# One load of keys in six pieces: 2,688 columns as one load, the last 1,408 as 112 rows and four loads of 4 rows

## The chip, the cores and the metric

The kernel runs on one core of a Trainium2 chip. The metric is the device time of one execution in microseconds (us). Three runs of the kernel before gave 237.23, 237.36 and 237.38 us, a median of 237.36 us. The profile shows one further execution of the same program.

## The reference

One decoding step of a transformer block for two sequences (B = 2, one token each, width 512), in 32-bit floats:

```python
mod = (silu(c) @ w_mod)                      # six vectors of 512 a sequence: sa, ca, ga, sb, cb, gb
h = layernorm(x) * (1 + ca) + sa
q = h @ wq                                   # 32 heads of 128
k, v = k_cache[:, :, -4096:, :], v_cache[:, :, -4096:, :]   # 8 key/value heads, each used by 4 heads
o = softmax(q k^T / sqrt(128)) v
x = x + ga * (o @ wo)
h = layernorm(x) * (1 + cb) + sb
x = x + gb * (silu(h @ w1) @ w2)             # hidden width 1792
```

Only the last 4,096 positions of the caches count. For each of the 8 key/value heads `h` and each of the two sequences `b` that is one block of keys and one of values, of 4,096 x 128 floats, 2 MB each: 32 blocks, 64 MB. The weights are `w_mod` (6 MB), `wq` and `wo` (8 MB each), `w1` and `w2` (3.5 MB each).

## The kernel before

Every large input comes through one pool of eight tiles of 128 x 4,096 floats (`ring`, line 55), and every load is issued by SyncE, in the order of the program: `w_mod` in four loads, `wq` in four, then keys and values head by head, `wo` in four, a load of 4 KB (`x_sp`), `w1` in three and `w2` in five, the last of them 512 columns (256 KB). A block of keys or values is one load of 128 rows of 16 KB (lines 77 to 89): 32 consecutive positions lie in one partition.

The function `fetch(h)` issues the loads of one step: the keys of head `h` for both sequences, and then the values of head `h - 1` for both. The first lines of the loop (447 to 451) call it one step ahead. So the loads around the change are `k2_0, k2_1, v1_0, v1_1, k3_0, k3_1, v2_0, v2_1, k4_0, k4_1, v3_0, v3_1`, where `k3_1` is the keys of head 3 of sequence 1.

SyncE issues a load when two things hold: the tile of the ring is free again (its last reader has run), and the semaphore that the load will count up has been reached by the load that used it before. There are eight such semaphores for loads, given out in turn, so a load waits for the completion of the load eight places ahead of it. SyncE is one queue: what stands behind a waiting load waits too.

A load of 128 rows is spread over the core's 16 DMA engines, eight rows each. Each engine works through its rows in the order of the issues and writes one completion for each load; the load has landed when all 16 completions are there.

For each head VectorE turns the keys (`keys`, line 333: a `k` tile in four parts of 1,024 columns, and `keys(h, b, n4)` reads the columns from 1,024 `n4` on), TensorE forms the scores (line 349), VectorE and ScalarE form maximum and exponentials, and TensorE multiplies the turned probabilities with the values (`weighted`, line 416). TensorE and VectorE each keep the order of the program there. Behind the heads follow the output projection with `wo`, the second norm, `w1`, `w2`, and the store of the result.

Of the kernel before, what the change touches and what calls it, by code (L numbers as in the profile page):

```python
# [13 lines left out]
P = 128  # L14
# [9 lines left out]
def adaln_block(  # L24
# [21 lines left out]
    nc = tc.nc  # L46
    SK = k_cache.shape[2]
    W = min(4096, max(256, SK // 4))
# [20 lines left out]
    def stream(name):  # L69
        return ring.tile([P, 4096], F32, tag="st", name=name)  # L70
# [5 lines left out]

    def load_k(b, h):
        t = stream(f"k{h}_{b}")
        nc.sync.dma_start(
            t, k_cache[b, h, SK - W :, :].rearrange("(p n) d -> p (n d)", p=P)  # L80
        )
        return t

    def load_v(b, h):
# [239 lines left out]
    def fetch(h):  # L324

        if h < HKV:
            for b in range(B):
                kt[h, b] = load_k(b, h)
        if h > 0:
            for b in range(B):  # L330
                vt[h - 1, b] = load_v(b, h - 1)
# [352 lines left out]
```

## Time and profile before

| what | value |
|---|---|
| median of three runs | 237.36 us |
| the profiled execution's own time | 236.89 us |
| its span, first to last instruction | 235.0 us |
| bytes read from HBM | 97.53 MB, 415 GB/s over the span |
| TensorE / VectorE / ScalarE busy | 62% / 49% / 11% |
| mean granted TensorE clock | 0.87 |

The page of the profile cuts the span into 40 slices of 5.9 us and gives for each the busy share of the engines, of the 16 DMA engines and the rate in GB/s. The chain of work that ended last goes back from the last instruction to what released it. Times in the views are microseconds from the start of the span. A load's row in the queue's view stands at its issue; it lands some 30 us later.

### The profile page before, as it was taken

What the parts mean: (1) busy time and instruction counts of PE and PEld (TensorE: products, weight loads), DVE (VectorE), ACT (ScalarE), POOL (GpSimd) and SP (SyncE); (2) the same over time, 40 slices, a digit from 0 to 9 for tenths busy, and PEclk for the clock granted to TensorE, in tenths of its full rate; (3) what the DMA queues carried; (4) which work ended last, traced back from release to release, by engine and by line L of the source; (5) the groups of instructions that cost most, each with busy time, mean ns of one, the idle gap of its engine ahead of it and who ended that gap; (6) DMA issues with size and microseconds to landing.
All of it is one profiled execution on the core that took longest, in us unless ns stands there. A gap on an engine that the chain in (4) does not pass through costs nothing.

```text
span 235.0 us, 2644 instructions
## 1 busy us (share of the span) xinstructions
PE 146.5 (62%) x1094; PEld 45.9 (20%) x1094; DVE 114.6 (49%) x176; ACT 25.4 (11%) x56; POOL 10.3 (4%) x30
## 2 busy tenths in 40 slices
PE   0086546367187577667549519626743967788993
PEld 0032101101011121121112102111211222335332
DVE  0634000793694792693892792595298050002130
ACT  2200000100300200200200200200020021003210
POOL 8600000100000000000000000000000000000000
PEclk9999975759869997999976967965985799999999
DMA  6999999999999999999999999999999999999991
GB/s 253 426 438 427 427 438 427 424 439 427 429 441 424 427 438 427 429 438 424 429 435 429 427 432 432 432 429 432 428 429 429 429 432 429 432 426 422 421 412 56
DMA packets 7603, 97.69 MB, mean 416 GB/s; under 512 B 920, under 2 KB 936, under 8 KB 1576
## 3 DMA queue, kind: packets, MB, share of 16 engines
q1 hardware_dynamic: 7592, 97.54, 97.5%
q8 instruction: 8, 0.13, 0.2%
q14 instruction: 3, 0.02, 0.0%
HBM read 97.53 MB, written 0.00 MB: 415 GB/s over the span
## 4 chain that ended last, share of the span: by engine, by line
DMA 64%; DVE 22%; PE 10%; ACT 2%; issue 1%; SPq 1%; DVEq 0%
DVE kT L337 16%; DMA wo<-in_A_wo_dram 14%; DMA k<-in_A_k_cache_dram 14%; DMA v<-in_A_v_cache_dram 13%; DMA wq<-in_A_wq_dram 13%; DMA w<-in_B_w_dram 7%; PE s L349 5%; DMA wm<-in_w_mod_dram 3%; DVE zp L395 2%; PE o L423 2%; PE q L285 1%; DVE xp L393 1%; ACT pr L381 1%; DVE mx L359 1%; ACT L381 1%
## 5 line engine op out<-in xcount | busy, mean ns | idle before, releaser
L337 DVE STREAM_TRANSPOSE kT<-k 128x1024 f32<-128x1024 f32 x64 | 73.7, 1210 | 1.6 <-DMA k<-in_A_k_cache_dram 1.6
L349 PE MATMUL s<-kT,qbd 128*32 128x512 f32 x256 | 44.5, 670 | 11.2 <-DVE kT L337 11.1
L423 PE MATMUL o<-v,ptb 128*32 128x512 f32 x256 | 38.5, 730 | 19.8 <-DMA v<-in_A_v_cache_dram 19.3
L359 DVE TENSOR_REDUCE mx<-s 128x1 f32<-128x512 f32 x8 | 5.5, 691 | 40.1 <-PE s L349 40.1
L349 PEld LDWEIGHTS s<-kT,qbd 128*32 128x32 f32 x256 | 11.1, 126 | 45.8 <-issue 24.1
L285 PE MATMUL q<-wq,hq_T 128*32 128x512 f32 x64 | 11.2, 836 | 10.1 <-DMA wq<-in_A_wq_dram 10.1
L423 PEld LDWEIGHTS o<-v,ptb 128*32 128x32 f32 x256 | 8.1, 124 | 35.8 <-issue 33.1
L402 PE MATMUL pT<-zp,id 128*32 128x256 f32 x64 | 5.6, 418 | 13.9 <-DVE zp L395 13.9
L379 ACT COPY bias<-bp 128x1 f32<-128x1 f32 x8 | 1.3, 159 | 111.9 <-PE bp L377 111.9
L537 PE MATMUL junk<-selh,id 128*32 128x256 f32 x46 | 11.3, 380 | 0.0
L294 DVE STREAM_TRANSPOSE qT<-q 128x512 f32<-128x512 f32 x2 | 1.4, 718 | 18.6 <-PE q L285 18.3
L395 DVE TENSOR_TENSOR zp<-xp,group 128x1024 f32<-128x1024 f32 x8 | 9.8, 1225 | 0.2
L393 DVE STREAM_TRANSPOSE xp<-pr 128x512 f32<-128x512 f32 x8 | 5.6, 701 | 4.4 <-ACT pr L381 4.4
L217 PE MATMUL mean_a<-mv_a,avg 128*128 128x1 f32 x2 | 0.6, 362 | 10.6 <-DVE mv_a L214 10.6
L361 PE MATMUL mT<-ident,mx 128*1 128x128 f32 x16 | 3.0, 270 | 6.4 <-DVE mx L359 6.4
L550 PE MATMUL acc_o<-wo,oTn 128*32 128x512 f32 x48 | 5.8, 598 | 1.9 <-DMA wo<-in_A_wo_dram 1.6
L537 PEld LDWEIGHTS junk<-selh,id 128*32 128x32 f32 x46 | 5.0, 110 | 6.7 <-issue 3.5
L438 PE MATMUL o_all<-ob,selh 128*64 128x128 f32 x64 | 5.7, 304 | 0.8 <-ACT ob L432 0.8
L270 DVE STREAM_TRANSPOSE xT<-x_sp 128x128 f32<-128x128 f32 x1 | 0.4, 403 | 11.8 <-DMA x_sp<-in_A_x_dram 11.8
L432 ACT COPY ob<-o 128x512 f32<-128x512 f32 x8 | 4.7, 585 | 10.3 <-PE o L423 10.3
L285 PEld LDWEIGHTS q<-wq,hq_T 128*32 128x32 f32 x64 | 2.1, 128 | 18.8 <-DMA wq<-in_A_wq_dram 12.5
L249 PE MATMUL m_sp<-wm,scT 128*32 128x512 f32 x32 | 5.7, 796 | 0.0
(132 smaller groups left out, 95.0 us busy)
## 6 DMA issues: line engine op xcount, KB each, us to landing
k<-in_A_k_cache_dram SPq DMA_DIRECT2D x16, 2048.0 KB, 30.2
v<-in_A_v_cache_dram SPq DMA_DIRECT2D x16, 2048.0 KB, 31.5
wq<-in_A_wq_dram SPq DMA_DIRECT2D x4, 2048.0 KB
wo<-in_A_wo_dram SPq DMA_DIRECT2D x4, 2048.0 KB, 32.3
wm<-in_w_mod_dram SPq DMA_DIRECT2D x4, 1536.0 KB, 10.2
w<-in_B_w_dram SPq DMA_DIRECT2D x2, 1024.0 KB, 23.2
w<-in_B_w_dram SPq DMA_DIRECT2D x1, 1792.0 KB
w<-in_B_w_dram SPq DMA_DIRECT2D x2, 896.0 KB
```

What stands on the lines that cost most here:

```text
L249: nc.tensor.matmul(m_sp[r, :], scT[:, k, :], cd[:, g], start=(k == 0), stop=(k == 3))
L285: nc.tensor.matmul(q_ps[n][32 * g : 32 * g + 32, :], hq_T[:, k, :], wv[:, n, g], start=(k == 0), stop=(k == 3),)
L337: inorder(nc.vector.transpose(kT[h, b][:, :, 8 * n4 : 8 * n4 + 8, :].rearrange("p j n k -> p n j k"), kt[h, b][:, n4 * 1024 : (n4 + 1) * 1 ...
L349: inorder(nc.tensor.matmul(s_ps[h][r : r + 32, :], qbd[h // 4][:, h % 4, b, j, :], kT[h, b][:, j, 16 * c : 16 * c + 16, :], start=(j == 0) ...
L359: inorder(nc.vector.tensor_reduce(mx, s_ps[h], axis=AX.X, op=ALU.max))
L393: inorder(nc.vector.transpose(xp, pr[h]))
L395: inorder(nc.vector.tensor_mul(zp, xp[:, None, :, 0:16].to_broadcast([P, 4, 16, 16]), group[:, :, None, None].to_broadcast([P, 4, 16, 16]),))
L402: inorder(nc.tensor.matmul(tp[32 * i : 32 * i + 32, :], id4, zp.rearrange("p a s x -> p (a s) x")[:, :, 4 * i : 4 * i + 4], start=True, st ...
L423: inorder(nc.tensor.matmul(o_ps[h][32 * c : 32 * c + 32, :], ptb[h % 2][:, 256 * b + 32 * w : 256 * b + 32 * w + 32], vt[h, b][:, 512 * w ...
L438: inorder(nc.tensor.matmul(o_all[r : r + 64, :], selh[:, m, HQ - G - G * h : 3 * HQ - G - G * h], o_sb[h][:, m * DH : (m + 1) * DH], start ...
L537: inorder(nc.tensor.matmul(junk[0:32, :256], id4, selh.rearrange("p m y -> p (m y)")[:, :256], start=True, stop=True,))
L550: inorder(nc.tensor.matmul(acc[32 * g : 32 * g + 32, :], oTn[:, q, :], wot[q // 8][:, q % 8, :], start=(q < 4), stop=(q >= 20),))
```

## The change

Only `load_k` changes, and only for `k3_1`. In place of one load of 128 rows x 4,096 columns, SyncE issues six loads into the same tile: 128 rows x 2,688 columns, then for the last 1,408 columns (5,632 bytes a row) 112 rows at once and the remaining 16 rows as four loads of four rows. Bytes, tile, and the order of everything else stay; the program's SyncE queue has five more loads, and each takes one of the eight semaphores.

```diff
     def load_k(b, h):
         t = stream(f"k{h}_{b}")
-        nc.sync.dma_start(
-            t, k_cache[b, h, SK - W :, :].rearrange("(p n) d -> p (n d)", p=P)
-        )
+        rows = k_cache[b, h, SK - W :, :].rearrange("(p n) d -> p (n d)", p=P)
+        if (h, b) != (3, 1):
+            nc.sync.dma_start(t, rows)
+            return t
+
+        c0 = 4096 - 1408
+        nc.sync.dma_start(t[:, :c0], rows[:, :c0])
+        cuts = (0, 112, 116, 120, 124, 128)
+        for p0, p1 in zip(cuts, cuts[1:]):
+            nc.sync.dma_start(t[p0:p1, c0:], rows[p0:p1, c0:])
         return t
```

## The prediction

> **What bounds the kernel now.** I read the page first, its slices and queues.
>
> ```profile
> span 235.0 us, 2644 instructions
> DMA  6999999999999999999999999999999999999991
> GB/s 253 426 438 427 427 438 427 424 439 427 429 441 424 427 438 427 429 438 424 429 435 429 427 432 432 432 429 432 428 429 429 429 432 429 432 426 422 421 412 56
> q1 hardware_dynamic: 7592, 97.54, 97.5%
> q8 instruction: 8, 0.13, 0.2%
> DMA 64%; DVE 22%; PE 10%; ACT 2%; issue 1%; SPq 1%; DVEq 0%
> x_sp<-in_A_x_dram SPq DMA_DIRECT2D x1, 4.0 KB
> ```
>
> The DMA engines are at 9 tenths or more from the second slice to the last but one. The table of stretches says the same with numbers (the last two columns are the busy share of the 16 DMA engines and GB/s):
>
> ```profile
> core 0: us, PE busy (x) PEld busy (x) DVE busy (x) ACT busy (x) POOL busy (x), PEclk, DMA share, GB/s
> 40.00:80.00 40.00, 24.08 (x128) 5.51 (x124) 26.91 (x36) 4.56 (x12) 0.94 (x4) 0.81 1.01 431
> 80.00:120.00 40.00, 26.41 (x192) 7.31 (x184) 29.16 (x31) 4.75 (x12) 0.00 (x0) 0.96 1.01 431
> 160.00:200.00 40.00, 27.58 (x212) 8.45 (x212) 17.78 (x25) 4.38 (x11) 0.00 (x0) 0.81 1.01 431
> ```
>
> 431 GB/s are 26.9 GB/s for each of 16 engines, whatever the compute does. A load of 2 MB takes 4.87 us, one of its 16,384-byte rows 0.608 us. A row of 5,632 bytes, the unit below, takes r = 0.209 us.
>
> What ends the run is the last row of the last DMA engine. The last 3 us of loading, in slices of 75 ns, and the chain with the queue behind it:
>
> ```profile
> DMA  9989997989897986857766474453544443320000
> DMA packets 283, 0.77 MB, mean 257 GB/s; under 512 B 41, under 2 KB 41, under 8 KB 283
> ```
> ```profile
> 213.97 16.51 DMA w<-in_B_w_dram
> 230.48 0.04 issue
> 230.53 1.10 PE acc_y L643 x24
> 231.66 0.30 DVE yo L653
> 231.98 0.29 DVE yo L654
> ```
> ```profile
> 231.16 0.16 PEld L643 LDWEIGHTS acc_y<-w,uT 128*32 128x32 f32 x8 [0.26 <-DMA w<-in_B_w_dram]
> 232.30 0.59 SPq L656 DMA_DIRECT2D out_dram<-yo  x1
> ```
>
> TensorE's last matmuls wait for the last load until 231.16, and nothing but a fixed tail follows. The busy share falls over about 2 us (228.8 to 230.7): the 16 engines don't finish together. The trace's DMA records give each engine's completion write (4 bytes). Offsets in ns from the first of a load's 16, sorted, for two loads of `wq`, for `k3_0`, for the last of `wo`, for `x_sp` (same zero as `wo`) and for the last load:
>
> ```
> wq[1]   0 52 227 235 252 340 375 396 399 468 541 549 577 589 628 657
> wq[2]   0 52 227 235 252 340 375 397 399 468 541 550 578 590 628 2072
> k3_0    0 52 227 236 252 340 376 399 469 541 550 578 590 1241 2049 2077
> wo[3]   0 227 340 375 399 549 589 821 1241 1463 1671 1892 1959 1993 2048 2076
> x_sp    280 393 428 1294
> last    0 280 399 428 549 821 938 1294 1464 1671 1892 1959 1993 2007 2048 2076
> ```
>
> Two things are to be seen. Offsets stand still for the whole run, so an engine that falls behind never catches up, and the end is set by the largest offset, 2.08 us. And one engine jumps from 657 to 2,072 just where the first of the eight 16-KB instruction fetches (the row q8) is read; the others jump later, one by one. `x_sp` has four completions, 52 or 53 ns behind offsets 227, 340, 375 and 1,241: a load whose outer size is 4 runs on four engines, and those four stand at 280, 428, 938 and 1,294 at the end, ahead of 2,076. I call them E.
>
> **The change, part by part.** *Bytes.* Each engine had eight rows of 16,384. Now all have eight of 10,752 and seven of 5,632 (112/16), and E gets one row of each four-row load: 4 more. So twelve engines lose one r (-0.209 us) and E gains 3r (+0.627 us). `x_sp` prices the pieces: 53 ns, of which its 1,024 bytes an engine take 38 at 26.9 GB/s, so 15 ns for two rows and a completion, 5 ns each. Twelve engines have 8 pieces more (+0.04), E 16 (+0.08). If rows cost only this, the twelve end at 2.08 - 0.17 = 1.91 us, E's last at 1.29 + 0.71 = 2.00: the end moves by -0.08 us.
>
> [...]
>
> *Where the rows are written.* This is what the free sum leaves out. In every 128-row load an engine has eight of 128 partitions, and the same ones each time. With 112 rows it has seven, so the division falls elsewhere, and rows go to partitions that another engine is filling at that moment from `k3_1`'s first part or, since offsets spread over 2.08 us (10r), already from `v2_0`. The four rows of a small load are neighbouring partitions written by all of E at about the same time. The trace of before has no such meeting of large rows. Bounds: from below, nothing, as `x_sp` suggests, whose eight scattered rows moved no other engine's offset (549, 821, 2,048, 2,076 unmoved), though with 512 bytes a row; a gain beyond -0.17 us is excluded, because the twelve lose no more bytes. From above, the small loads' rows each wait for four other writers (5r each), the 112-row load's for one (2r): 14r + 20r = 34r on E in place of 8r, +5.43 us, and with +0.08 and E's 1.29 an end at 6.80 us, +4.7. The nearest row of two streams in one another's way is the fetch: 16 KB that alone take 0.608 us set an engine back by 2,072 - 657 = 1.42 us, 2.3 times. So I take one other writer for each moved row, 2r: E has 22r for 8r, +2.93 + 0.08 = 3.01 us, and ends at 1.29 + 3.01 = 4.30, the twelve at 2.08 + 6r + 0.04 = 3.37. The end moves by 4.30 - 2.08 = +2.2 us. If only the small loads meet another writer, E has 15r, +1.54 us, ends at 2.83: +0.8.
>
> [...]
>
> *The queue.* Five more issues, each taking a semaphore.
>
> ```profile
> 0.73 0.40 SPq L74 DMA_DIRECT2D wm<-in_w_mod_dram  x1
> ...
> 68.55 1.76 SPq L79 DMA_DIRECT2D k<-in_A_k_cache_dram  x2
> 73.05 7.95 SPq L86 DMA_DIRECT2D v<-in_A_v_cache_dram  x2
> 85.21 4.83 SPq L79 DMA_DIRECT2D k<-in_A_k_cache_dram  x2
> 90.13 9.19 SPq L86 DMA_DIRECT2D v<-in_A_v_cache_dram  x2
> ```
> ```profile
> 90.13 31.36 DMA v<-in_A_v_cache_dram
> ```
> ```profile
> 102.18 1.92 PE L423 MATMUL o<-v,ptb 128*32 128x512 f32 x16 [0.72 <-DMA v<-in_A_v_cache_dram]
> ```
> ```profile
> 100.00 8.00 DVE L337 STREAM_TRANSPOSE kT<-k 128x1024 f32<-128x1024 f32 x7
> ```
>
> `v2_0` lands at 102.2, where TensorE waits for it; one load is 4.87 us, so `k3_1` lands at 97.3, `k3_0` at 92.4, `v1_1` at 87.6. With six loads in `k3_1`'s place the small loads wait for `v0_1`, `k2_0`, `k2_1` and `v1_0` (82.7), and behind them `v2_0` for `v1_1`: `v2_0`, issued at 73.05 now, goes at 87.6, `v2_1` behind `k3_0` at 92.4, `k4_0` and `k4_1` behind pieces of `k3_1` at 95 to 101, in place of 85.2 and 90; `v3_1`, at some 99, hardly moves. At 87.6 the queue still holds `k3_0` and `k3_1`, 9.7 us, less the 2.1 us by which the first engine leads: 7.6 us of cover, so the stall costs nothing. Without it, each us late is a us of idle DMA.
>
> *Readers.* VectorE turns the tile in the last four of seven parts from 100.00 on, so from 103.4: 6.1 us behind `k3_1`'s landing, which covers 3. `v2_0`, next in the same rings, has no cover: TensorE waits at 102.18 already. That shifts head 3 by up to 3 us, frees buffers as much later, and the loads in flight hide it (a load of values issued at 90.13 takes 31.36 us to land, six loads' time). It isn't added: the same lag arrives at the end anyway.
>
> *Sum.* Profiled execution: 236.89 + 2.2 = 239.1 us. The median shown is 0.47 higher: 237.36 + 2.2 = 239.6 us.
>
> **The rivals.** *A: moved rows are free.* The change then does what the offsets allow: it fills the four early engines and relieves the twelve, -0.08 us, 237.3. For it: an unmoved 431 GB/s, and `x_sp`. Against: 512-byte rows are too short to tell. E has 0.08 us to spare over eleven rows: it is no slower up to 1.03r a row, and within 0.2% up to 1.24r.
> *B: all of E meets on each four-row load.* +4.7 us, 242.1. For it: four rows in the same four neighbouring partitions, and three of E stand within 0.15 us of each other. Against: the first collision spreads them, and then they follow one another.
> *C: the semaphores empty the queue.* If a load takes 10 us from issue to first byte, the DMA engines idle for 10 - 7.6, +2.4 us, 239.8. Against: the first load of all, issued at 0.73, is moving within the first slice of 5.9 us, which shows 253 GB/s.
> *D: the four-row loads aren't spread over E.* One engine with all 16 rows gains 15r, 3.1 us; even from offset 0 that ends at 3.2 us, +1.1, 238.5. Against: `x_sp`'s four completions.
>
> **How the numbers follow.** Forecast (one other writer, +0.8 to +3.3): 0.50. B: 0.17, A: 0.19, C: 0.05, D: 0.05, a gain that I see no place for: 0.04. Why A is below the forecast: it needs all of eleven rows to meet nobody, and the only meeting in the trace cost 2.3 times its bytes. [...] A measurement of this kernel can tell about 0.2%, 0.47 us, from no change. Slower takes forecast, B, C and most of D: 0.75. Within 0.2%: A and a rest of D, 0.19. Faster: 0.06. The range goes from A, 237.2, to 241.2, which leaves out B's upper part (0.12) and gains beyond 237.2 (0.05). The slow cases' own range is 238.1 to 242.1.
>
> **What would show it.** Completion offsets behind `k3_1`: E up by some 3 us and the twelve by 1.3 (forecast), or E by 0.71 and the twelve by -0.17 (A). The rate in 92 to 107 us: a dip below 430 GB/s, or none. The fall of the busy share at the end: over some 4.3 us instead of 2.1, or a little steeper. The last weight load's wait: to 233.4, or 231.1. For C: `v2_0`'s issue at 87.6, and a gap in the DMA share behind it. Wrong it would be, above all, if DMA engines can write into each other's partitions at full rate, or if rows wait for several others; and if the five more instructions move an instruction fetch onto an engine that is already late, which adds up to 1.4 us to any case.

## The result, and the profile after

The changed kernel takes 239.63 us (median of five runs, 239.44 to 240.03) beside 237.29 us for the kernel before (237.10 to 237.38): a ratio of 1.0102, interval 1.0088 to 1.0116, so 2.3 us or 1.0% slower. The profiled execution took 239.44 us with a span of 237.5 us; before it was 236.89 and 235.0.

The page of the changed kernel, the same rows as before:

```profile
span 237.5 us, 2652 instructions
DMA  7999999999999999999999999999999999999991
GB/s 248 426 437 420 436 433 433 421 431 433 436 428 425 431 433 388 307 425 431 436 428 431 431 428 433 428 432 436 420 436 431 428 431 433 428 427 420 427 409 63
q1 hardware_dynamic: 7752, 97.54, 97.6%
DMA 73%; PE 11%; DVE 11%; ACT 2%; issue 1%; SPq 1%; DVEq 0%
```

Bytes are the same to the last digit, and the DMA engines are busy in every slice. But two slices, 15 and 16 counted from 0 (89 to 101 us), move 388 and 307 GB/s in place of some 430. That is where the pieces of `k3_1` pass. The table of stretches of the changed kernel, with the same busy share of the DMA engines throughout (second number from the end):

```profile
80.00:95.00 15.00, 11.23 (x72) 2.74 (x64) 9.56 (x10) 0.96 (x2) 0.00 (x0) 0.89 1.01 414
95.00:110.00 15.00, 9.47 (x64) 3.49 (x68) 12.08 (x13) 1.90 (x5) 0.00 (x0) 0.78 1.01 379
110.00:125.00 15.00, 7.37 (x65) 2.55 (x61) 11.49 (x13) 1.90 (x5) 0.00 (x0) 0.84 1.01 431
```

The kernel before, in the first two of them:

```profile
80.00:95.00 15.00, 11.28 (x72) 2.65 (x64) 9.65 (x9) 0.96 (x2) 0.00 (x0) 0.89 1.00 428
95.00:110.00 15.00, 9.62 (x79) 3.04 (x82) 12.09 (x13) 1.90 (x5) 0.00 (x0) 1.00 1.01 433
```

So the DMA engines did not wait. They were busy for as long and moved less: 14 and 54 GB/s less over 15 us each are 1.0 MB, or 2.4 us at 431 GB/s. SyncE's queue in the changed kernel:

```profile
69.95 0.33 SPq L85 DMA_DIRECT2D k<-in_A_k_cache_dram  x1
70.33 12.27 SPq L88 DMA_DIRECT2D k<-in_A_k_cache_dram  x5
87.25 5.22 SPq L93 DMA_DIRECT2D v<-in_A_v_cache_dram  x2
96.88 2.71 SPq L81 DMA_DIRECT2D k<-in_A_k_cache_dram  x2
99.68 0.86 SPq L93 DMA_DIRECT2D v<-in_A_v_cache_dram  x2
```

and TensorE, which waits for `v2_0` until 104.37 (102.18 before), and at the end for the last load until 233.75 (231.16 before):

```profile
104.37 3.64 PE L430 MATMUL o<-v,ptb 128*32 128x512 f32 x16 [2.97 <-DMA v<-in_A_v_cache_dram]
...
233.75 0.16 PEld L650 LDWEIGHTS acc_y<-w,uT 128*32 128x32 f32 x8 [0.26 <-DMA w<-in_B_w_dram]
```

So 2.2 us are lost by `v2_0`, and 2.6 at the end. The completion writes of the 16 engines in the DMA records, in ns, sorted. The zero is the first engine at `k3_0`, carried on at the undisturbed 4.862 us a load, so that a row shows how far the engines have fallen behind:

```
before  v2_0    0 52 227 236 252 340 375 399 468 541 550 578 590 1241 2049 2077
after   k3_0    0 65 244 267 378 512 520 571 597 651 677 684 733 1055 1439 1651
after   v2_0    1907 1910 2604 2855 2862 2908 2917 2919 2948 2993 3010 3143 3327 3329 3640 4019
after   wo[3]   1907 2496 2604 2862 2908 2917 2948 3327 3329 3640 4018 4275 4422 4429 4430 4563
after   x_sp    2970 3001 3380 4071
```

Between `k3_0` and `v2_0` every one of the 16 falls behind, by 2.33 us on average. From there to `wo[3]` ten of the offsets stand still to within 1 ns; six engines jump, one by 0.59 us and five by 1.44 on average, and one instruction fetch of 8 KB and five of 16 KB fall into that time. The last engine stands at 4,563 ns where it stood at 2,076 before: 2.49 us, and the span is 2.5 us longer.

### The profile page after: what moved, and what is told of

It reads as the page before. It is cut to its first block, busy times and chain, and to the rows that moved or that the text cites. A ratio compares the mean times of both kernels' runs of the same rounds, so it can differ in the third digit from the quotient of the medians.

```text
span 237.5 us, 2652 instructions
## 1 busy us (share of the span) xinstructions
PE 147.4 (62%) x1094; PEld 46.8 (20%) x1094; DVE 114.7 (48%) x176; ACT 25.4 (11%) x56; POOL 10.3 (4%) x30
## 4 chain that ended last, share of the span: by engine, by line
DMA 73%; PE 11%; DVE 11%; ACT 2%; issue 1%; SPq 1%; DVEq 0%
DMA v<-in_A_v_cache_dram 25%; DMA wo<-in_A_wo_dram 14%; DMA wq<-in_A_wq_dram 13%; DMA k<-in_A_k_cache_dram 12%; DVE kT L344 7%; DMA w<-in_B_w_dram 7%; PE o L430 4%; PE s L356 3%; DMA wm<-in_w_mod_dram 3%; PE q L292 1%; DVE zp L402 1%; ACT pr L388 1%; DVE xp L400 1%; DVE mx L366 1%; ACT L388 1%
## 5 line engine op out<-in xcount | busy, mean ns | idle before, releaser
L430 PE MATMUL o<-v,ptb 128*32 128x512 f32 x256 | 39.8, 754 | 23.7 <-DMA v<-in_A_v_cache_dram 23.2
L356 PE MATMUL s<-kT,qbd 128*32 128x512 f32 x256 | 42.7, 671 | 8.9 <-DVE kT L344 8.9
L356 PEld LDWEIGHTS s<-kT,qbd 128*32 128x32 f32 x256 | 11.7, 126 | 41.6 <-issue 24.2
L557 PE MATMUL acc_o<-wo,oTn 128*32 128x512 f32 x48 | 7.2, 730 | 1.8 <-DMA wo<-in_A_wo_dram 1.4
```

Source lines behind the costliest of these rows:

```text
L356: inorder(nc.tensor.matmul(s_ps[h][r : r + 32, :], qbd[h // 4][:, h % 4, b, j, :], kT[h, b][:, j, 16 * c : 16 * c + 16, :], start=(j == 0) ...
L430: inorder(nc.tensor.matmul(o_ps[h][32 * c : 32 * c + 32, :], ptb[h % 2][:, 256 * b + 32 * w : 256 * b + 32 * w + 32], vt[h, b][:, 512 * w ...
L557: inorder(nc.tensor.matmul(acc[32 * g : 32 * g + 32, :], oTn[:, q, :], wot[q // 8][:, q % 8, :], start=(q < 4), stop=(q >= 20),))
```

## The experiments

All were run beside the kernel before; its medians were 236.90 us (experiments 1 to 4), 237.06 (5 to 8) and 237.17 (9 and 10).

| run | what | median us | ratio, interval |
|---|---|---|---|
| e1 | 2,688 and 1,408 columns, both 128 rows | 237.06 | 1.0008 (0.9998 to 1.0017) |
| e2 | `k3_1` whole, four more four-row loads, partitions 0 to 15 | 236.84 | 0.9996 (0.9987 to 1.0006) |
| e9 | the same, partitions 32 to 47 | 237.00 | 0.9996 (0.9987 to 1.0006) |
| e10 | the same, partitions 16 to 31 | 238.10 | 1.0040 (1.0026 to 1.0054) |
| e4 | the same, partitions 64 to 79 | 238.30 | 1.0070 (1.0046 to 1.0093) |
| e3 | the same, four neighbours at a time, 112 to 127 | 237.84 | 1.0042 (1.0028 to 1.0057) |
| e5 | the change, four-row loads on partitions 0 to 15 | 238.70 | 1.0074 (1.0053 to 1.0094) |
| e6 | the change, last 16 rows as one load | 239.74 | 1.0111 (1.0096 to 1.0126) |
| e7 | last 1,408 columns as two loads of 64 rows | 240.62 | 1.0158 (1.0131 to 1.0184) |
| e8 | the change with 2,816 columns | 243.34 | 1.0260 (1.0243 to 1.0277) |

What the profiled execution of each but e8 shows in its DMA records, for rows that start between 84 and 105 us, where the pieces pass: the number of rows and their mean time, and the time of all of them above the undisturbed 215 and 611 ns:

```
             5,632-byte rows       16,384-byte rows      both, above undisturbed
before       -                     553, mean 611 ns      0.0 us
after        128, mean 356 ns      362, mean 653 ns      33.1 us (36.2 with the 10,752-byte rows)
e1           128, mean 215 ns      422, mean 611 ns      0.0 us
e2            16, mean 215 ns      542, mean 611 ns      0.0 us
e9            16, mean 215 ns      545, mean 611 ns      0.0 us
e10           16, mean 291 ns      521, mean 639 ns      15.6 us
e4            16, mean 272 ns      525, mean 634 ns      13.2 us
e3            16, mean 267 ns      522, mean 637 ns      14.2 us
e5           128, mean 344 ns      367, mean 647 ns      29.6 us
e6           128, mean 346 ns      375, mean 645 ns      29.4 us
e7           128, mean 429 ns      329, mean 684 ns      51.5 us
```

**Cutting alone (e1).**

```diff
-        cuts = (0, 112, 116, 120, 124, 128)
-        for p0, p1 in zip(cuts, cuts[1:]):
-            nc.sync.dma_start(t[p0:p1, c0:], rows[p0:p1, c0:])
+        nc.sync.dma_start(t[:, c0:], rows[:, c0:])
```

> The last 1,408 columns as one load of 128 rows instead of five loads: each DMA engine keeps the partitions that it has in every other load. Theory 1 (moved rows meet the engine that fills the same partitions): no row moves, eight pieces more an engine at 5 ns, so within 0.1 us of before, no packet of 5,632 bytes over some 215 ns. Rival 2 (cutting the load and taking more semaphores costs): a clear part of the 2.3 us, 0.4 us or more for one of five cuts.

Measured: +0.16 us, with an interval that holds no change, and not one row slower. Each of the 16 engines stands 43 or 44 ns later behind the pieces, as the 5 ns a piece have it. The cut is not the cause.

**Four more loads of four rows, in five places (e2, e9, e10, e4, e3).** `k3_1` is loaded whole, and 16 rows of it once more into a spare tile that nothing reads. Between the five runs only the 16 rows differ, and with them the partitions that are written: `sl` picks both the rows that are read and the partitions.

```diff
+        spare = stream("spare")
+        for j in range(4):
+            sl = slice(j, 16, 4)            # e2; e9: slice(32 + j, 48, 4); e10: slice(16 + j, 32, 4)
+                                            # e4: slice(64 + j, 80, 4); e3: slice(112 + 4 * j, 116 + 4 * j)
+            nc.sync.dma_start(spare[sl, :1408], rows[sl, 4096 - 1408 :])
```

> [...] Theory 1: four engines have 4r + 0.06 = 0.90 us more work and meet nobody; they stand at 1.29 at the end, so +0.1 us, and the other offsets don't move. Rival 2 (four-row loads are dear in themselves, wherever they write): as much as the next run, over +1 us.

> k3_1 whole, and the four more four-row loads to partitions 32+j, 36+j, 40+j, 44+j of the spare tile. [...] If only the first 16 partitions are cheap, or neighbouring partitions: +0.9 to +1.4 us, as with partitions 64 to 79.

> [...]

> [...] Theory 1: each row meets one other writer, so the four engines fall back 8r + 0.06 = 1.73 us and end at 3.02, +0.9 us, and four others fall back 4r = 0.84 us, at most to 2.92. Rival 2: the same as the two runs before.

> As the run before it, but the four loads write partitions 112 to 115, 116 to 119, 120 to 123 and 124 to 127, as in the change. Theory 1: the four engines meet each other and a fifth on each load, 16r to 20r, 3.4 to 4.2 us, and end at 4.7 to 5.5: +2.6 to +3.4 us if they all meet, +0.9 us (8r) if they spread. Rival 2: the same time as with the other partitions.

The completion offsets of e2, before and behind its four loads (ns):

```
e2  k3_0   0 13 22 33 275 277 286 358 467 477 570 600 653 1161 1850 2039
e2  v2_0   0 13 22 33 357 467 476 569 600 653 1146 1147 1156 1849 2032 2039
```

Four engines (275, 277, 286 and 1,161) go to 1,146, 1,147, 1,156 and 2,032, each by 870 or 871 ns, 218 for each of four rows with its completion. The twelve others don't move by more than 1 ns. In e9 four engines move by 870 or 871 ns as well. The same of e10, where no engine stays where it was:

```
e10 k3_0   0 35 49 155 240 277 372 479 583 623 737 856 894 1252 2112 2206
e10 v2_0   951 962 1072 1374 1484 1520 1529 1631 1758 1791 1985 2018 2110 3007 3169 3468
```

The stretch from 95 to 110 in e2, e9, e10 and e4, in this order; all four load as many bytes:

```profile
95.00:110.00 15.00, 9.70 (x78) 3.00 (x82) 12.04 (x13) 1.90 (x5) 0.00 (x0) 1.00 1.00 428
```
```profile
95.00:110.00 15.00, 9.62 (x76) 2.88 (x79) 12.08 (x13) 1.90 (x5) 0.00 (x0) 1.00 1.00 427
```
```profile
95.00:110.00 15.00, 9.86 (x72) 3.36 (x76) 11.56 (x13) 1.90 (x5) 0.00 (x0) 0.77 1.01 404
```
```profile
95.00:110.00 15.00, 7.37 (x60) 2.13 (x56) 10.09 (x10) 1.48 (x4) 0.00 (x0) 0.77 1.00 405
```

This shows that the place decides. Sixteen small rows cost nothing in partitions 0 to 15 and 32 to 47, and 0.9 to 1.4 us in 16 to 31, 64 to 79 and 112 to 127; a row took 215 ns on average in the first two places and 291, 272 and 267 in the others. Nearness to partition 0 is not what counts: 16 to 31 lie nearer to it than 32 to 47. What is dear is not a small load, not its four engines, not its semaphores, but the place of its rows. That the dear places are those which another DMA engine fills in the 128-row loads was the author's estimate; the DMA records name no partitions. Whether the write counts or the reading of other rows is not shown either: `sl` picks both. The TensorE clock, 0.77 in the two slow stretches, is not the cause: the kernel before moves 431 GB/s at a clock of 0.81 from 160 to 200 us.

But the delay is not one between the engine that has such a row and one other, as in the expectation for e4, where four engines and four others fall back. In e10 thirteen engines stand below 900 ns at `k3_0` and none below 951 at `v2_0`. Eight of the twelve engines without a small load can be followed row by row there, and each fell behind by 0.89 to 0.92 us. Three of the four with small loads fell behind by 1.74 us, of which 0.87 are their own rows as in e2: they lost no more than the others. The 16 moved rows lost 1.2 us in all, the rows of 16,384 bytes 14.4 us, on all 16 engines between about 95.4 and 99 us. In e4 the smallest offset goes from 0 to 755 ns, in e3 from 0 to 818.

The queue is ruled out too. SyncE's queue in e2 shows four small loads and late issues behind them, as in the change:

```profile
72.98 5.38 SPq L88 DMA_DIRECT2D spare<-in_A_k_cache_dram  x4
82.65 5.20 SPq L93 DMA_DIRECT2D v<-in_A_v_cache_dram  x2
92.44 5.17 SPq L81 DMA_DIRECT2D k<-in_A_k_cache_dram  x2
```

`v2_0` goes at 82.65 in place of 73.05, and the time does not change.

e4 was expected at +0.9 us and cost 1.40. Its profiled execution was its slowest, 239.75 us beside 238.10 to 238.53 for the other four; in it one engine goes from 2,862 to 4,954 ns and ends the run. e3, four neighbours at once, cost 0.94 us (the intervals of the two overlap), which is the time expected if its rows spread and not that of a full meeting; its 16 rows took 267 ns on average, where a meeting of all four engines and a fifth would take an estimated 1,075 (5 x 215).

**Which part of the change carries it (e5, e6).**

```diff
-        cuts = (0, 112, 116, 120, 124, 128)
-        for p0, p1 in zip(cuts, cuts[1:]):
-            nc.sync.dma_start(t[p0:p1, c0:], rows[p0:p1, c0:])
+        nc.sync.dma_start(t[16:, c0:], rows[16:, c0:])                       # e5
+        for j in range(4):                                                   # e5
+            nc.sync.dma_start(t[j:16:4, c0:], rows[j:16:4, c0:])             # e5
+        nc.sync.dma_start(t[:112, c0:], rows[:112, c0:])                     # e6
+        nc.sync.dma_start(t[112:, c0:], rows[112:, c0:])                     # e6
```

> The change with the four-row loads moved to the rows that cost nothing beside a whole k3_1: rows j, 4+j, 8+j, 12+j, and the 112-row load on rows 16 to 127. What is left of the 2.3 us is the 112-row load's. If the four-row loads carried the change, as the prediction had it (its four engines end last): little is left, under 0.8 us. If the displaced rows of the 112-row load carry it: 1.5 to 2.3 us. Cutting alone was shown to cost nothing, so without meetings: 0.

> The last 16 rows as one load, one row for each of the 16 engines, so that no engine gets more bytes than before. Theory 1: seven displaced rows at 2r and one into partitions 112 to 127, where 16 engines and four owners meet (about 5r): 19r for 8r, 2.3 us for all engines, +1.5 to +2.8 us. If the gain in bytes of the four engines were the cause instead: 0.

With the four-row loads where they are free, +1.64 us remain beside the 2.34 of the change (the intervals overlap a little): the 112-row load carries most of it. With no four-row load at all and no engine given more bytes, it is +2.68 us. So the larger share of the four engines is not what lengthens the run.

**Two halves (e7), and twice the columns (e8).**

```diff
-        cuts = (0, 112, 116, 120, 124, 128)
-        for p0, p1 in zip(cuts, cuts[1:]):
-            nc.sync.dma_start(t[p0:p1, c0:], rows[p0:p1, c0:])
+        for p0 in (0, 64):                                                   # e7
+            nc.sync.dma_start(t[p0 : p0 + 64, c0:], rows[p0 : p0 + 64, c0:]) # e7
```
```diff
-        c0 = 4096 - 1408
+        c0 = 4096 - 2816                                                     # e8
```

> The last 1,408 columns as two loads of 64 rows, partitions 0 to 63 and 64 to 127: 16 engines with four rows each, no small load, no engine with more bytes. [...] If only displaced or small rows cost: 0 to 0.8 us.

> The change with 2,816 columns in place of 1,408: every row that is moved is twice as long, the number of loads is the same. Theory 1: the time in meetings doubles, +4.0 to +5.0 us. Rival (a fixed cost per moved row or load): +2.3 us.

e7 has one load more than e1, even shares and no small load, and is the dearest form of these 1,408 columns: +3.56 us. Its rows took 429 ns on average, twice the undisturbed 215; and the rows of 16,384 bytes, which were not moved, took 684 in place of 611 and added 24 us of engine time, 1.5 us an engine. e8 costs +6.28 us, 2.7 times the change and above its expected 4 to 5 us: a fixed cost for each load is ruled out, and why it is more than double is not shown. Its rows of 11,264 bytes took 783 ns on average, the fastest 422. Their stretches from 95 to 110:

```profile
95.00:110.00 15.00, 7.39 (x54) 2.30 (x56) 12.09 (x13) 1.89 (x5) 0.00 (x0) 0.81 1.01 352
```
```profile
95.00:110.00 15.00, 4.59 (x44) 1.64 (x46) 11.51 (x12) 1.90 (x5) 0.00 (x0) 0.75 0.99 299
```

No version beat the kernel before: e2 and e9 load 90 KB more at no cost, but give no time back.

## Why the prediction was right, and where not

**Bound and place.** Right: the run ends with the last row of the last DMA engine, offsets stay, and 2.49 us of lost offset became 2.5 us of span.

**Moved rows meet another engine, 2r each.** Right that the place of a row decides, as e2 and e9 against e10, e4 and e3 show, and near in size: the 5,632-byte rows took 356 ns on average, 1.7 times their 215. Wrong in the mechanism. The prediction lets a moved row wait for one other writer and delays nothing else; in e10 and e4 rows that nobody moved are slow on all 16 engines, and the moved rows have 1.2 of the 15.6 us and 0.9 of the 13.2. No record names the partitions that an engine writes: that a moved row meets one other engine at its partitions was the author's estimate, and so are the fifth engine that e3's expectation counts and the four owners that e6's counts. What the runs show is a mean of 267 ns for the 16 extra rows of e3 and of 346 for the 128 rows of e6, beside 215.

**E's end, 4.30 us.** Near for the last of them: the four engines that run `x_sp` end at 2.97, 3.00, 3.38 and 4.07. That the four-row loads of `k3_1` run on these four is not shown; e2 shows four engines that move by 870 or 871 ns each.

**The twelve's end, 3.37 us.** Here a step failed, and the sum came out right all the same. The sum for them has only the delay of their own moved rows. The rows of 16,384 bytes, which nobody moved, lost 15.2 us of engine time in the changed kernel, up to 1,320 ns for one of 611; the 10,752-byte rows 3.1; the moved rows 18.0. So the twelve fell back by 2.1 to 2.3 us on average (their offsets at `v2_0` average 2,840, at `k3_0` between 575 and 723, by which engines one takes for E) in place of the 1.29 predicted. One of them, not E, ends the run: it left `v2_0` at 3,143, and a 16-KB fetch of 1.42 us brought it to 4,563. That the predicted 2.2 us met the measured 2.34 is so far luck, of an oversized term and one that was missing: the engine taken for the last stood 0.23 us less late than predicted, and another 0.49 us later than it. One of the prediction's signs failed with this step: the engines were to finish over 4.3 us instead of 2.1, but the earliest fell behind too, and at `wo[3]` the 16 stand within 2.7 us (1,907 to 4,563).

**The queue.** Right: `v2_0` was issued at 87.25 (87.6 predicted), the next loads at 96.88 and 99.68, the DMA share stayed at 1.01, and e2 has a stall of the same kind, to 82.65, for nothing.

**Readers.** Right: TensorE waited 2.97 us for `v2_0` (0.72 before), and the loss at the end, 2.6 us, is no more than the engines' lateness.

**The rivals.** A, moved rows are free, fell with e10, e4 and e3; why the 512-byte rows of `x_sp` show nothing of it was not tested. B, all of E meeting on each four-row load, fell with e3: +0.94 us, not the 2.6 to 3.4 expected of a full meeting. C, an empty queue, fell with the changed kernel's own trace, where the DMA share is 1.01 behind the late issue, and with e2. D fell with e2: four engines moved, by four rows each. The four-row loads alone have the smaller part: e3 has just these four loads and costs 0.94 us, and e5 leaves 0.7 of the 2.34 us to them.

## What to carry to other kernels

Here loads bound the kernel (431 GB/s before and after, away from the pieces), the last DMA engine ended it, at 2,076 ns before and 4,563 after, and an engine once late stayed late; but handing its share to another engine row by row cost 2.34 us. In these runs 16 rows of 5,632 bytes at partitions 16 to 31, 64 to 79 or 112 to 127 slowed the whole stream: the 16-KB rows that nobody moved took 634 to 639 ns on average in place of 611. Keep loads at 128 rows, and cut by columns if at all (e1: +0.16 us, within the noise). Loads of four rows were free beside the stream at partitions 0 to 15 and 32 to 47 (e2 and e9, both 0.9996) and cost 0.93 to 1.40 us at the three other places; which places are free, two runs on different partitions tell at once.

## What the runs showed of the hardware that was not expected

Sixteen rows in the wrong place slowed all 16 engines. In e3, e4 and e10 the completion offsets of all engines together grow by 17.1, 16.6 and 19.0 us from `k3_0` to `v2_0`, of which 3.5 are the 16 extra rows themselves. The rest is 0.82 to 0.97 us for each row, where by the prediction's estimate of one other writer a row of 0.21 us would delay itself and that engine by 0.42 together, and leave the others alone. How a row comes to delay engines that did not load it is not known from these runs.
